# First layer norm with its root on ACT, transposes copied by two engines, matmuls on ones ahead of it, x transposes one V group later

## The chip, the cores and the metric

The kernel runs on one core of one Trainium2 chip. The metric is device microseconds of one execution, without the launch; lower is better.

Engines: PE does matmuls and transposes, PEld is its weight load, DVE is VectorE, ACT is ScalarE, POOL is GpSimd, SP issues the DMAs. A bank is a part of the buffer that PE writes to; in this kernel ACT or DVE copies it out ("evicts" it) before PE fills it again. The granted clock is the share of PE's full clock that the profile records.

## The reference, cut to what matters

The reference is a recurrent memory transformer block followed by a gated MLP with spatial mixing. Only its opening matters here: x is layer-normalized, and from it the projections Q, K and V are taken.

```python
def _layernorm(x, axis=-1, eps=1e-05):
    m = jnp.mean(x, axis=axis, keepdims=True)
    v = jnp.var(x, axis=axis, keepdims=True)
    return (x - m) / jnp.sqrt(v + eps)
# ... in _A_ref, for each of 64 segments of 32 tokens:
    h = jnp.concatenate([mem, xs], axis=1)
    q = jnp.einsum('btd,dhe->bhte', h, Wq)      # D = 512, 32 heads of 128
    k = jnp.einsum('btd,dhe->bhte', h, Wk)
    v = jnp.einsum('btd,dhe->bhte', h, Wv)
# ... main:
x = A_x
h = x + _A_ref(_layernorm(x, axis=-1), ...)
h2 = h + _B_ref(_layernorm(h, axis=-1), ...)
```

## The kernel before: the parts that matter

The program has a start, which projects the rows that every segment needs in advance; a main loop over 64 segments; and the MLP. The change edits the start alone. Its inputs are two 128-row blocks, x0 (`load_xe(0, 0)`) and x1 (`load_xe(1, 1)`), and the three weights, each 4 MB in four quarters. All of the program's DMAs stand in one queue (q1 on the page, 72.26 MB), in this order: x0, x1, four quarters of Wq, some more x, four of Wv, four of Wk.

```python
def ln_stats(j):                         # DVE: statistics; POOL: (var + eps) ** -0.5
    t, tok = xbuf(j); k = j % 3
    dve(... e.bn_stats(out=st1[:, k, :], in_=t) ...)                                     # L364
    dve(... e.bn_aggr(out=mv1[:, k, :], in_=st1[:, k, :]) ...)                           # L365
    pool(... e.tensor_scalar(out=rs1[:, k:k + 1], in0=mv1[:, k, 1:2], scalar1=EPS, op0=ALU.add) ...)   # L366
    pool(... e.tensor_tensor(out=rs1[:, k:k + 1], in0=rs1[:, k:k + 1], in1=mhalf[:, 0:1], op=ALU.pow) ...)  # L368
def ln_apply(j):                         # DVE: (x - mean) * rstd, in place               # L374
def xT(j, bank):                         # PE: four 128x128 transposes into one bank      # L384
def xe_copy(ck, bank):                   # ACT: that bank to hTe[ck]                      # L409
def qkx_mm(ck, i, bank):                 # PE: a group of 16 matmuls on hTe[ck] and Wq/Wk # L426
def vx_mm(ck, n, bank):                  # PE: a V group on Wv                            # L461

act(lambda e: e.preload_act_table_set("natural_log_exp_and_others"))
for j in range(2):
    ln_stats(j)
for j in range(2):
    ln_apply(j)
    xT(j, 6 + j)
    xe_copy(j, 6 + j)
# ... loads of Wv and Wk
def start_group(mm, ev, *a):             # one group into one of 4 banks; evicted by ACT and DVE in turn
    ...
for i in range(8):                       # "Q phase": 16 groups, x0 and x1 in turn
    for ck in range(2):
        start_group(qkx_mm, qkx_evac, ck, i)
    if i == 6:
        for j in range(4, 7):
            ln_stats(j)
        late_consts()
for n in range(8):                       # "V phase": 8 groups of x0
    if n < 3:
        ln_apply(n + 4)
    start_v(0, n)
    if n == 1: xT(4, 6); ring_copy(0, 6)
    if n == 2: xT(5, 7); ring_copy(1, 7)
    if n == 3: xT(6, 6); xe_copy(2, 6); mem0_transpose(7); load_wo(0)
# ... then 8 groups of K, 8 of V (x1), 8 of K; then the main loop
```

The recording layer gives each engine its instructions in this order, and in the traces each engine starts them in it: in after x1 has landed at 4.11 us, but DVE starts its statistics at 6.20, behind x0's half copy (5.99). In the changed kernel the lines move: L374 becomes L378, L384 L388, L409 L413, L426 L431, L436 L441, L461 L466.

The softmax here doesn't subtract the row's maximum and nothing guards it: scores larger than these inputs give would overflow.

## Time and profile before

| what (first trace of before) | us |
|---|---|
| time, median of the first 3 runs | 876.12 (875.36 to 876.2) |
| span of the trace (this execution took 871.85) | 870.1 |
| PE busy | 848.3 |
| first matmul of the Q phase | 7.8 |
| Q phase, to the first V group | 15.8 |
| V phase, to the first K group | 9.08 |
| first matmul of the main loop | 54.19 |

These are lines of the page of before: busy time by engine (us, share of the span, instructions), busy tenths in 40 slices of the span, and the chain that ended last.

```profile
PE 848.3 (97%) x22453; PEld 431.5 (50%) x18869; DVE 502.1 (58%) x1245; ACT 467.4 (54%) x1291; POOL 158.2 (18%) x427
...
PE   6999999999999999999999999999999999999997
...
PE 96%; DVE 2%; issue 1%; DMA 0%; ACT 0%; POOL 0%; SPq 0%
```

PE is the bound, and apart from the last slice, where the work runs out, only its first slice has a hole. This is the timeline of the start of before (start and length in us, engine, line, operation, output<-input, count; in brackets how long the engine had been idle and what ended it):

```profile
4.47 0.22 POOL L366 TENSOR_SCALAR f_rs<-f_mv 128x1 f32<-128x1 f32 x1 [2.91 <-DVE f_mv L365]
...
4.78 0.57 POOL L368 TENSOR_TENSOR f_rs<-f_rs,f_mhalf 128x1 f32<-128x1 f32 x1
...
5.58 0.38 DVE L374 TENSOR_SCALAR f_xn<-f_xn,f_mv,f_rs 128x512 bf16<-128x512 bf16 x1
...
6.01 0.61 PE L384 MATMUL f_ps<-f_ident,f_xn 128*128 128x128 bf16 x4 [6.01 <-DVE f_xn L374]
...
6.66 0.60 ACT L409 ACTIVATE f_hTe<-f_ps 128x512 bf16<-128x512 bf16 x1 [4.59 <-PE f_ps L384]
```

Read alone, this says that PE waits 6 us for the layer norm. It hides the other input of the first group. In the trace's DMA records, the last part of Wq's first quarter lands at 7.67 us, while x0's copy has ended by 7.26. In the second trace of before the PE timeline itself names the DMA:

```profile
6.99 0.61 PE L384 MATMUL f_ps<-f_ident,f_xn 128*128 128x128 bf16 x4 [0.58 <-DVE f_xn L374]
7.90 16.28 PE L426 MATMUL f_ps<-f_hTe,f_arena 128*128 128x128 bf16 x256 [0.31 <-DMA f_arena<-in_A_Wq_dram]
```

Last, PE's wait in the V phase of before, in PE's timeline:

```profile
23.59 1.91 PE L461 MATMUL f_ps<-f_arena,f_hTe 128*32 128x512 bf16 x32
25.98 0.40 PE L384 MATMUL f_ps<-f_ident,f_part 128*128 128x128 bf16 x4 [0.48 <-DVE f_part L374]
```

### The profile page before, as it was taken

Reading aid. Unit: us, or ns where it says so; the run is one execution under the profiler, and the core shown is the slowest. Engines: PE = TensorE matmul, PEld = TensorE weight load, DVE = VectorE, ACT = ScalarE, POOL = GpSimd, SP = SyncE. Lnnn points to the kernel's source line nnn. Section 1 sums busy time; section 2 is a strip of 40 time slices with the busy share of each in tenths; the row PEclk is TensorE's granted clock in tenths of the full one; section 3 lists DMA queues with packets and bytes.
Section 4 is the critical chain, followed back from the end, with each engine's and each line's share of the span. In section 5 each row is a group of like instructions: output and inputs, shape, how many; then the busy total and the mean of one; then the engine's idle time right before and its main releaser. Section 6 shows DMA issues by size and latency. Waiting matters only on the chain.

```text
span 870.1 us, 45443 instructions
## 1 busy us (share of the span) xinstructions
PE 848.3 (97%) x22453; PEld 431.5 (50%) x18869; DVE 502.1 (58%) x1245; ACT 467.4 (54%) x1291; POOL 158.2 (18%) x427
## 2 busy tenths in 40 slices
PE   6999999999999999999999999999999999999997
PEld 6664545544455445554445445555454444444443
DVE  3446666666666666666666666666565554634443
ACT  3446666766666666656666666666666655200000
POOL 1712112121121212121122112121111122100000
PEclk9999999999999999999999999999999999999999
DMA  9972232213031222222241323333221870033001
GB/s 326 379 215 71 76 63 74 66 38 86 25 92 41 67 57 37 72 67 73 62 91 27 81 65 67 95 55 74 51 62 41 209 253 1 0 110 108 26 13 38
DMA packets 114038, 75.22 MB, mean 86 GB/s; under 512 B 70696, under 2 KB 99376, under 8 KB 113840
## 3 DMA queue, kind: packets, MB, share of 16 engines
q1 hardware_dynamic: 113840, 72.26, 30.1%
q8 instruction: 164, 2.69, 1.3%
q14 instruction: 34, 0.28, 0.1%
HBM read 39.46 MB, written 20.58 MB: 69 GB/s over the span
## 4 chain that ended last, share of the span: by engine, by line
PE 96%; DVE 2%; issue 1%; DMA 0%; ACT 0%; POOL 0%; SPq 0%
PE f_ps L280 30%; PE f_ps L660 13%; PE f_ps L281 13%; PE f_ps L1090 11%; PE f_ps L710 3%; PE f_ps L426 3%; PE f_ps L461 3%; PE f_ps L1052 3%; PE f_ps L1083 3%; PE f_ps L1161 3%; PE f_ps L574 3%; PE f_ps L625 3%; PE f_ps L631 1%; PE f_ps L554 1%; PE f_ps L681 1%
## 5 line engine op out<-in xcount | busy, mean ns | idle before, releaser
L280 PE MATMUL f_ps<-f_arena,f_hT 128*32 128x512 bf16 (+1 forms) x5120 | 352.8, 337 | 1.7 <-issue 0.6
L281 PE MATMUL f_ps<-f_arena,f_hT 128*32 128x256 bf16 (+1 forms) x3072 | 214.5, 308 | 0.0
L280 PEld LDWEIGHTS f_ps<-f_arena,f_hT 128*32 128x32 bf16 x5120 | 121.1, 96 | 169.0 <-issue 85.6
L518 ACT ACTIVATE f_Tst<-f_ps 128x512 bf16<-128x512 f32 (+1 forms) x320 | 149.9, 510 | 57.8 <-PE f_ps L280 54.1
L660 PE MATMUL f_ps<-f_arena,f_cT 128*32 128x256 bf16 x4096 | 133.5, 273 | 1.1 <-ACT f_cT L645 1.1
L597 POOL TENSOR_TENSOR f_E_sb<-f_R_sb,f_E_sb 128x64 bf16<-128x64 f32 x128 | 48.1, 376 | 378.2 <-ACT f_R_sb L589 378.2
L526 DVE STREAM_TRANSPOSE f_QT<-f_Tst 128x256 uint32<-128x256 uint32 x128 | 57.0, 446 | 94.9 <-ACT f_Tst L518 94.9
L660 PEld LDWEIGHTS f_ps<-f_arena,f_cT 128*32 128x32 bf16 x4096 | 92.0, 95 | 34.8 <-ACT f_cT L645 21.2
L1090 PE MATMUL f_ps<-f_arena 128*128 128x512 bf16 x448 | 101.3, 379 | 2.5 <-DVE f_arena L1096 1.6
L617 DVE TENSOR_SCALAR f_V_sb<-f_ps 128x512 bf16<-128x512 f32 (+1 forms) x128 | 70.6, 551 | 41.0 <-PE f_ps L280 41.0
L672 ACT ACTIVATE f_part<-f_ps 128x256 bf16<-128x256 f32 x128 | 49.2, 384 | 66.5 <-PE f_ps L660 66.5
L647 DVE TENSOR_SCALAR f_cT<-f_ps 128x160 bf16<-128x160 f32 (+1 forms) x192 | 61.0, 373 | 38.4 <-PE f_ps L631 38.4
L645 ACT ACTIVATE f_cT<-f_ps 128x160 bf16<-128x160 f32 (+1 forms) x192 | 53.0, 348 | 39.4 <-PE f_ps L631 39.4
L1090 PEld LDWEIGHTS f_ps<-f_arena 128*128 128x128 bf16 x448 | 43.6, 98 | 55.9 <-DVE f_arena L1096 2.6
L526 DVE STREAM_TRANSPOSE f_KT<-f_Tst 128x128 uint32<-128x128 uint32 (+1 forms) x192 | 66.0, 356 | 2.7
L585 ACT ACTIVATE f_R_sb<-f_ps 128x160 f32<-128x160 f32 x128 | 38.9, 304 | 33.6 <-PE f_ps L281 26.5
L1096 DVE TENSOR_TENSOR f_arena<-f_ps,f_arena 128x512 f32<-128x512 f32 x28 | 19.3, 690 | 57.8 <-PE f_ps L1090 57.8
L567 ACT ACTIVATE f_E_sb<-f_ps 128x224 bf16<-128x224 f32 x128 | 45.7, 357 | 0.0
L593 DVE TENSOR_TENSOR f_E_sb<-f_R_sb,f_E_sb 128x160 bf16<-128x160 f32 x128 | 44.7, 349 | 0.0
L589 ACT ACTIVATE f_R_sb<-f_R_sb 128x160 f32<-128x160 f32 x128 | 42.6, 333 | 2.0
L710 PE MATMUL f_ps<-f_arena,f_cTx 128*32 128x512 bf16 x512 | 40.5, 380 | 0.0
L280 PE MATMUL f_ps<-f_arena,f_hTe 128*32 128x512 bf16 x512 | 39.0, 382 | 0.0
(105 smaller groups left out, 1024.1 us busy)
## 6 DMA issues: line engine op xcount, KB each, us to landing
wT_d<-f_wst SPq DMA_DIRECT2D x32, 256.0 KB, 2.0
f_arena<-wT_d SPq DMA_DIRECT2D x32, 256.0 KB, 4.8
f_arena<-in_A_Wq_dram SPq DMA_DIRECT2D x4, 1024.0 KB
f_arena<-in_A_Wv_dram SPq DMA_DIRECT2D x4, 1024.0 KB
f_arena<-in_A_Wk_dram SPq DMA_DIRECT2D x4, 1024.0 KB, 15.9
f_arena<-in_A_Wo_dram SPq DMA_DIRECT2D x4, 1024.0 KB
f_Vx<-vext_d SPq DMA_DIRECT2D x128, 32.0 KB
f_xn<-in_A_x_dram SPq DMA_DIRECT2D x16, 128.0 KB, 2.2
```

What stands on the lines that cost most here:

```text
L280: return e.matmul(out, lhsT=lhsT, rhs=rhs, start=start, stop=stop, skip_group_check=True, tile_position=pos)
L281: return e.add_instruction(mybir.InstMatmult(name=nc.get_next_instruction_name(), engine=mybir.EngineType.PE, ins=[e.lower_ap(rhs), e.lowe ...
L518: act(lambda e: e.activation(out=st_.rearrange("p (hp i r) -> p hp i r", i=32, r=2), in_=ps[:, bank, 0:64 * np_].rearrange("p (hp r i) -> ...
L526: dve(lambda e: e.transpose(out=dst, in_=src), reads=tok, writes=[(nm, b, k) for k in halves(b, p0, np_)])
L597: pool(lambda e: e.tensor_tensor(out=ev, in0=rv, in1=ev, op=ALU.mult), reads=[("R", b), ("Ex", b)], writes=[("Ex", b)])
L617: dve(lambda e: e.tensor_scalar(out=dst, in0=src, scalar1=VSC, scalar2=None, op0=ALU.mult), reads=[PB(bank)], writes=tok)
L645: act(lambda e: e.activation(out=dst, in_=src, func=ACT.Copy, scale=UNSC), reads=[PB(PVB[c])], writes=tok)
L647: dve(lambda e: e.tensor_scalar(out=dst, in0=src, scalar1=UNSC, scalar2=None, op0=ALU.mult), reads=[PB(PVB[c])], writes=tok)
L660: pe(lambda e, h=h, g=g, i=i, b=b, c=c: e.matmul(ps[32 * g:32 * g + 32, bank, 0:d1 - d0], lhsT=cTh[:, i, 8:40], rhs=w_o[:, h, d0:d1], star ...
L672: act(lambda e: e.activation(out=part[:, s % 8, d0:d1], in_=ps[:, bank, 0:d1 - d0], func=ACT.Copy), reads=[PB(bank)], writes=[("part", s % ...
L710: pe(lambda e, h=h, g=g, i=8 * qr + bg: e.matmul(ps[32 * g:32 * g + 32, WXB, :], lhsT=cTx[:, rb % 2, i, :], rhs=w_o[:, h, :], start=(i < 4 ...
L1090: pe(lambda e: e.matmul(ps[:, bank, 0:TB], lhsT=z2[:, sc, fb * 128:(fb + 1) * 128], rhs=wTb[tb % 2][:, :, sc, :], start=(sc == 0), stop=(s ...
```

## The change

The intent is to start PE's real work earlier and on a fast clock: a shorter root for x0's layer norm (the root is (var + eps) ** -0.5, here as Ln and Exp on ACT in place of an addition and a power on POOL), its transposes copied in halves by ACT and DVE, 40 matmuls on ones while PE would idle, and x1's layer norm moved behind x0's so that x0 goes first. Separately, the transposes in the V phase come one group later.

```diff
-    def ln_stats(j):
+    def ln_stats(j, on_act=False):
...
+        if on_act:
+            act(lambda e: e.activation(out=rs1[:, k:k + 1], in_=mv1[:, k, 1:2], func=ACT.Ln, bias=EPS), ...)
+            act(lambda e: e.activation(out=rs1[:, k:k + 1], in_=rs1[:, k:k + 1], func=ACT.Exp, scale=-0.5), ...)
+            return
...
-    for j in range(2):
-        ln_stats(j)
-    for j in range(2):
-        ln_apply(j)
-        xT(j, 6 + j)
-        xe_copy(j, 6 + j)
+    for _ in range(40):
+        pe(lambda e: e.matmul(ps[:, 5, 0:128], lhsT=onesrc[:, 0:128], rhs=onesrc[:, 0:128], start=True, stop=True), ...)
+    ln_stats(0, True)
+    ln_apply(0)
+    xT(0, 6, (0, 1))
+    xT(0, 7, (2, 3))
+    act(lambda e: e.activation(out=hTe[:, 0, 0:2, :], in_=psb[:, 6, 0:256]..., func=ACT.Copy), ...)
+    dve(lambda e: e.tensor_copy(out=hTe[:, 0, 2:4, :], in_=psb[:, 7, 256:512]...), ...)
+    ln_stats(1, True)
+    ln_apply(1)
...
             start_group(qkx_mm, qkx_evac, ck, i)
+            if ck == 0 and i == 0:
+                xT(1, 1)
+                xe_copy(1, 1)
...
-        if n == 1:
+        if n == 2:
             xT(4, 6)
...                                     # likewise n == 2 -> 3 and n == 3 -> 4
```

The rest of the diff splits the dependency token of `hTe` into two halves.

More of the change, by code (lines that the diff above doesn't have):

```diff
@@ L365, in ln_stats @@
         dve(lambda e: e.bn_aggr(out=mv1[:, k, :], in_=st1[:, k, :]), reads=[("st1", k)], writes=[("mv1", k)])
+        if on_act:
+            act(lambda e: e.activation(out=rs1[:, k:k + 1], in_=mv1[:, k, 1:2], func=ACT.Ln, bias=EPS), reads=[("mv1", k)], writes=[("rs1", k)])
+            act(lambda e: e.activation(out=rs1[:, k:k + 1], in_=rs1[:, k:k + 1], func=ACT.Exp, scale=-0.5), reads=[("rs1", k)], writes=[("rs1", k)])
+            return
         pool(lambda e: e.tensor_scalar(out=rs1[:, k:k + 1], in0=mv1[:, k, 1:2], scalar1=EPS, scalar2=None, op0=ALU.add),
@@ L379, in ln_inplace, with xT @@
         ln_apply(j)
-    def xT(j, bank):
+    def xT(j, bank, dcs=range(DC)):
         t, tok = xbuf(j)
-        for dc in range(DC):
+        for dc in dcs:
             pe(lambda e, dc=dc: e.transpose(out=psb[:, bank, dc * 128:(dc + 1) * 128], in_=t[:, dc * 128:(dc + 1) * 128],
@@ L393, in x_flip @@
         sp(lambda e: e.dma_start(xs_d[i], t), reads=rd, writes=[("xs", i)])
-        sp(lambda e: e.dma_start_transpose(out=dst, in_=xs_d[i]), reads=[("xs", i)], writes=[tok])
+        sp(lambda e: e.dma_start_transpose(out=dst, in_=xs_d[i]), reads=[("xs", i)], writes=tok)
     def ring_fill(rb):
@@ L408, in xe_copy @@
         src = psb[:, bank, 0:512].rearrange("p (dc c) -> p dc c", dc=DC)
-        act(lambda e: e.activation(out=hTe[:, ck % 3, :, :], in_=src, func=ACT.Copy), reads=[PB(bank)], writes=[("hTe", ck % 3)])
+        act(lambda e: e.activation(out=hTe[:, ck % 3, :, :], in_=src, func=ACT.Copy), reads=[PB(bank)],
+            writes=[("hTe", ck % 3, 0), ("hTe", ck % 3, 1)])
     def mem0_transpose(bank):
@@ L427, in qkx_mm @@
                                                          rhs=hTe[:, ck % 3, dc, :], start=(dc == 0), stop=(dc == DC - 1)),
-                   reads=[("hTe", ck % 3), ("W", mi, q // 2)], writes=[PB(bank)])
+                   reads=[("hTe", ck % 3, dc // 2), ("W", mi, q // 2)], writes=[PB(bank)])
     def qkx_evac(ck, i, bank, eng="act"):
@@ L445, in qkx_rows @@
                                           dc == 0, dc == DC - 1, (0, 32 * c)),
-               reads=[("hTe", ck % 3), ("W", mi, 2 * b), ("W", mi, 2 * b + 1)], writes=[PB(bank)])
+               reads=[("hTe", ck % 3, dc // 2), ("W", mi, 2 * b), ("W", mi, 2 * b + 1)], writes=[PB(bank)])
     def qkx_flip(ck, mi, r, b, bank):
@@ L462, in vx_mm @@
                                                        start=(dc == 0), stop=(dc == DC - 1), tile_position=(0, 32 * c)),
-                   reads=[("hTe", ck % 3), ("W", 2, n // 2)], writes=[PB(bank)])
+                   reads=[("hTe", ck % 3, dc // 2), ("W", 2, n // 2)], writes=[PB(bank)])
     def vx_evac(ck, n, bank, eng="act"):
@@ L758, in fast_path @@
     act(lambda e: e.preload_act_table_set("natural_log_exp_and_others"))
-    for j in range(2):
-        ln_stats(j)
-    for j in range(2):
-        ln_apply(j)
-        xT(j, 6 + j)
-        xe_copy(j, 6 + j)
+    for _ in range(40):
+        pe(lambda e: e.matmul(ps[:, 5, 0:128], lhsT=onesrc[:, 0:128], rhs=onesrc[:, 0:128], start=True, stop=True), reads=["onesrc"], writes=[PB(5)])
+    ln_stats(0, True)
+    ln_apply(0)
+    xT(0, 6, (0, 1))
+    xT(0, 7, (2, 3))
+    act(lambda e: e.activation(out=hTe[:, 0, 0:2, :], in_=psb[:, 6, 0:256].rearrange("p (dc c) -> p dc c", dc=2), func=ACT.Copy),
+        reads=[PB(6)], writes=[("hTe", 0, 0)])
+    dve(lambda e: e.tensor_copy(out=hTe[:, 0, 2:4, :], in_=psb[:, 7, 256:512].rearrange("p (dc c) -> p dc c", dc=2)),
+        reads=[PB(7)], writes=[("hTe", 0, 1)])
+    ln_stats(1, True)
+    ln_apply(1)
     for mi in (2, 1):
@@ L797, in fast_path @@
         start_v(0, n)
-        if n == 1:
+        if n == 2:
             xT(4, 6)
             ring_copy(0, 6)
-        if n == 2:
+        if n == 3:
             xT(5, 7)
             ring_copy(1, 7)
-        if n == 3:
+        if n == 4:
             xT(6, 6)
@@ L985, in fast_path @@
         if j4 == 1 and 2 <= rb + 2 < RB:
-            late.append(lambda rb=rb: (ln_apply(0), x_flip(0, rb, xn[:, 1, :].rearrange("p (dc c) -> p dc c", dc=DC), ("xn", 1))))
+            late.append(lambda rb=rb: (ln_apply(0), x_flip(0, rb, xn[:, 1, :].rearrange("p (dc c) -> p dc c", dc=DC), [("xn", 1)])))
         if s == 2:
@@ L989, in fast_path @@
         if s == 3:
-            late.append(lambda: (ln_apply(7), x_flip(7, RB, hTe[:, 0, :, :], ("hTe", 0))))
+            late.append(lambda: (ln_apply(7), x_flip(7, RB, hTe[:, 0, :, :], [("hTe", 0, 0), ("hTe", 0, 1)])))
         if j4 == 1 and rb >= 2:
```

## The prediction

> **What bounds the kernel now.** The chain of waits gives PE 96% of the span, and PE is busy 848.3 of 870.1 us. The change touches only the first 33 us. There the timeline shows three losses:
> - PE starts at 6.01 us with transposes of x0; the first projection matmul (L426) starts at 7.80.
> - PE starts slow: L426 matmuls are 107 ns apart until 10.75 us and 56 ns after it. 28 of them are slow, about 28 x 51 ns = 1.4 us. [...]
> - In the V phase PE waits 0.5 us (25.5 to 26.0) for DVE's layer norm of part.
>
> **The hidden floor.** x0's transposes are copied by 7.26 us, but the trace's DMA landings put the first quarter of Wq at 7.67, and PE's wait for it ends at 7.75. So L426 already starts on the weights, not on the layer norm. Later quarters leave little room: Wk's first lands at 31.54, its users start at 32.67.
>
> **What the change does.** The POOL pair (0.22 + 0.57 us and gaps, 4.47 to 5.35) becomes Ln and Exp on ACT, estimated at 0.2 us each from the 0.19 us of a 128x32 ACTIVATE: saves about 0.4 us. With fast transposes and two half copies (about 0.4 us, estimated from the 0.60 us copy) x0's hTe is ready near 6.3 instead of 7.26. That is off the critical path: Wq lands near 7.7.
>
> The 40 matmuls on ones fill about 1.1 to 5.4 us (40 x 107 ns) and should warm PE. Near 764 us a 1.8 us idle stretch leaves later matmuls at 216 ns, so idling to 7.7 should not cool it. Then the first group takes 0.9 us (7.8 to 8.7), not 1.6.
>
> But x1 is now late: its statistics stand behind DVE's half copy (about 6.35), so it is normalized near 8.3 and transposed after the first group, near 8.9. Its copy (0.60) stands on ACT behind the first group's eviction (0.74 us, 8.9 to 9.65), so the second group starts near 10.3 and issues its last matmul near 11.2; before it was 10.93. So a new PE wait eats the warm clock's 1.4 us, and the Q phase ends 0.0 to 0.4 us later.
>
> V phase: x transposes a group later remove the 0.5 us wait: 9.08 us (23.59 to 32.67) becomes about 8.5. Wk (31.54) then just does not bind.
>
> The rest is PE-bound and merely shifts. [...]a 0.86 us "issue" gap at 61.2 may come or go.
>
> **Sum.** -1.4 (clock) + 1.6 (new wait) - 0.55 (V phase) = about -0.35 us: 875.7 us (8 in 10: 873.8 to 877.2). Chances: faster by over 2% 0.01, within 2% 0.98, slower by over 2% 0.01.
>
> **What would show it.** First L426 still near 7.8: floor right. 56 ns apart from there: warming right. A PE gap of over 1 us before the second L426 group, released by ACT's hTe copy: new wait right. No wait of L384 on DVE near 25 us: V phase right. Start of the main loop (54.19 before) near 53.9.
>
> **What would make it wrong.** PE cooling again in the idle stretches (about 0.9 us slower); weights landing earlier (up to 1 us more gain, until Wk binds); [...]run-to-run spread (0.8 us before).

What the first trace of before shows: PE has work from 7.20 us, and its matmuls are 107 ns apart until 10.75 and 56 ns after it; later PE idles for 1.80 us ahead of L1041 (765.73), and the matmuls that follow are 216 ns apart, as before the idle stretch.

## More of the kernel before

The windows view gives busy time with counts, and the granted clock, in any stretch. For before, up to 10.77 us and after it (columns: stretch and length; PE, PEld, DVE, ACT, POOL busy with counts; clock, DMA share, GB/s):

```profile
7.36:10.77 3.41, 3.41 (x33) 3.17 (x32) 0.00 (x0) 1.34 (x2) 0.00 (x0) 1.00 1.05 394
10.77:14.18 3.41, 3.41 (x64) 3.41 (x63) 1.46 (x2) 1.05 (x2) 0.00 (x0) 1.00 1.05 386
```

In the first stretch 33 matmuls are under way, in the second 64: one every 107 ns, then one every 56 ns. The clock column says 1.00 for both, because this trace's clock record begins only with the first switch, at 10.77; before it one has to look at the matmuls.

## The result, and the profile after

Six runs of the changed kernel: median 876.96 us (875.3 to 879.15); before, in the same rounds and those of the first measurement: 875.74 (872.86 to 876.2). A ratio is the mean time of one kernel's fast runs over that of the other's in the same rounds, so it is not quite the ratio of these medians. It is 1.0023, with a 95% interval of 1.0001 to 1.0045: within 2%, and slower by some 2 us (0.1 to 3.9) where 0.4 us faster was foretold. The median lies inside the foretold range, but before was itself quicker in these rounds: set against the 876.12 from which the prediction started, the ratio stands for 878.1. A second measurement (below) gave 1.0036.

The timeline of the start of after, first trace:

```profile
1.07 4.45 PE L765 MATMUL f_ps<-f_onesrc 128*128 128x128 bf16 x40 [1.07 <-POOL f_onesrc L328]
...
4.37 0.20 ACT L367 ACTIVATE f_rs<-f_mv 128x1 f32<-128x1 f32 x1 [2.30 <-DVE f_mv L365]
4.60 0.20 ACT L368 ACTIVATE f_rs<-f_rs 128x1 f32<-128x1 f32 x1
...
5.32 0.63 PE L388 MATMUL f_ps<-f_ident,f_xn 128*128 128x128 bf16 x4
...
5.99 0.29 DVE L772 COPY f_hTe<-f_ps 128x256 bf16<-128x256 bf16 x1 [0.74 <-PE f_ps L388]
6.20 0.68 DVE L364 BATCH_NORM_STATS2 f_st<-f_xn 128x6 f32<-128x512 bf16 x1
...
8.15 1.05 PE L431 MATMUL f_ps<-f_hTe,f_arena 128*128 128x128 bf16 x16 [2.20 <-DMA f_arena<-in_A_Wq_dram]
...
9.04 0.39 PE L388 MATMUL f_ps<-f_ident,f_xn 128*128 128x128 bf16 x4
...
9.24 0.74 ACT L441 ACTIVATE f_arena<-f_ps 128x512 bf16<-128x512 f32 x1 [1.67 <-PE f_ps L431]
9.84 0.58 ACT L413 ACTIVATE f_hTe<-f_ps 128x512 bf16<-128x512 bf16 x1
10.47 2.58 PEld L431 LDWEIGHTS f_ps<-f_hTe,f_arena 128*128 128x128 bf16 x25 [1.22 <-ACT f_hTe L413]
```

Four things stand there. The root takes two times 0.20 us on ACT, and x0's two half copies end near 6.3 us, about 1 us before the 7.26 of before. The first group gains nothing from it: it starts at 8.15, after 2.2 us of idling, when Wq has landed (8.01 in this run). The first group is fast: 16 matmuls and four transposes start between 8.15 and 9.2. And then PE waits for x1: its statistics came after x0's half copy on DVE, its transposes after the first group on PE, its copy after that group's eviction on ACT.

The V phase is as hoped; in PE's timeline of after there is no wait ahead of L388:

```profile
25.34 2.77 PE L466 MATMUL f_ps<-f_arena,f_hTe 128*32 128x512 bf16 x48
28.05 0.40 PE L388 MATMUL f_ps<-f_ident,f_part 128*128 128x128 bf16 x4
```

But it begins at 25.34, against 23.59 before. The windows view of after shows why the wait for x1 is not the whole of it:

```profile
3.14:6.55 3.41, 2.81 (x27) 2.49 (x24) 1.85 (x5) 0.79 (x3) 0.00 (x0) 1.00 1.00 305
6.55:9.96 3.41, 1.28 (x20) 1.13 (x20) 0.92 (x3) 1.13 (x4) 0.00 (x0) 1.00 1.05 400
9.96:13.38 3.42, 2.91 (x28) 2.91 (x29) 0.73 (x1) 0.46 (x2) 0.00 (x0) 0.50 1.05 387
13.38:16.79 3.41, 3.41 (x64) 3.41 (x62) 1.01 (x2) 1.50 (x2) 0.00 (x0) 1.00 1.06 369
```

The warm-up got the fast clock, at 6.55. The next 3.41 us held PE busy for only 1.28 us, and the clock was halved for the 3.41 us after them, in which 28 matmuls are counted where the following stretch counts 64. Before, which never warms up early, has its 28 slow matmuls while it waits for nothing; after has 27 slow ones anyway, later, and the wait on top.

### The profile page after: what moved, and what is told of

Same layout as the page of the kernel before. It is cut to its first block, busy times and chain, and to the rows that moved or that the text cites. A ratio compares the mean times of both kernels' runs of the same rounds, so it can differ in the third digit from the quotient of the medians.

```text
span 875.9 us, 45517 instructions
## 1 busy us (share of the span) xinstructions
PE 855.7 (98%) x22486; PEld 437.4 (50%) x18909; DVE 502.7 (57%) x1246; ACT 467.9 (53%) x1295; POOL 156.8 (18%) x423
## 4 chain that ended last, share of the span: by engine, by line
PE 96%; DVE 1%; issue 1%; DMA 1%; ACT 0%; SPq 0%; POOL 0%
PE f_ps L280 30%; PE f_ps L665 13%; PE f_ps L281 13%; PE f_ps L1104 11%; PE f_ps L431 3%; PE f_ps L466 3%; PE f_ps L715 3%; PE f_ps L1066 3%; PE f_ps L1097 3%; PE f_ps L579 3%; PE f_ps L1175 3%; PE f_ps L630 3%; PE f_ps L636 1%; PE f_ps L559 1%; PE f_ps L686 1%
```

## The experiments

**Two readings to tell apart.** Theory T: after loses because the clock that the 40 matmuls bought is taken back while PE idles. Theory X: it loses because x1 comes late. Besides, the first pair of traces differed by 5.8 us of span, of which only 1.2 us stood at the start of the main loop; so theory P (the 80 added PE instructions move the main loop's stalls) and its rival N (noise of single runs) had to be told apart too.

All traces, in us. "Slow" counts Q-phase matmuls recorded 107 ns apart instead of 56. The time from the first K group to the main loop was 21.52 us (to 0.01) in every trace.

| trace | first group | Q phase | slow | V phase | loop starts | loop start to L1041* | L1041* to end |
|---|---|---|---|---|---|---|---|
| before | 7.81 | 15.78 | 28 | 9.08 | 54.19 | 711.6 | 104.4 |
| before again | 7.91 | 16.21 | 37 | 9.08 | 54.72 | 711.7 | 104.9 |
| before, third | 7.68 | 16.96 | 51 | 9.08 | 55.24 | 712.6 | 104.5 |
| after | 8.15 | 17.20 | 27 | 8.53 | 55.41 | 714.5 | 106.0 |
| after again | 7.69 | 18.59 | 55 | 8.54 | 56.34 | 711.0 | 104.3 |
| after, third | 7.58 | 18.36 | 50 | 8.54 | 56.00 | 712.9 | 104.4 |
| no warm | 8.12 | 17.97 | 43 | 8.54 | 56.16 | 709.9 | 104.3 |
| warm only | 7.83 | 14.38 | 0 | 9.57 | 53.30 | 712.3 | 106.0 |
| after, filled | 8.08 | 15.84 | 0 | 8.54 | 53.98 | 714.0 | 106.5 |
| x1 early | 8.01 | 16.01 | 33 | 8.53 | 54.08 | 713.1 | 104.5 |
| V shift only | 8.33 | 16.74 | 47 | 8.54 | 55.13 | 713.1 | 104.5 |
| pool root | 8.04 | 19.37 | 70 | 8.54 | 57.47 | 714.0 | 104.7 |
| pool root again | 7.76 | 17.38 | 31 | 8.54 | 55.21 | 713.5 | 104.8 |
| x1 early, filled | 7.76 | 14.38 | 0 | 9.94 | 53.60 | 713.9 | 104.3 |

*L1041 is the one matmul of the finiteness check in the MLP, at 765.74 us in before; its line differs in the other kernels.

### 1 and 2. Both kernels against themselves

No edit. Five rounds each, on one chip with 3 and 4.

> The kernel before, unchanged, against itself. It tells how far two traces and two times of the same program differ. Theory P[...]: the time from the first main-loop matmul to the start of the last phases repeats within 0.5 us of the first trace of before (54.19 us to about 684.7 us), and the single stalls (0.86 us near 61.2, 0.97 us near 558.9) stand at the same places. Rival N (run-to-run noise): loop time differs by 1 us or more and the stalls move. Both: ratio 1.000, main loop starts at 54.2 +-0.3 us.

> The changed kernel once more. Main loop starts at 55.4 +-0.5 us if PE again falls back to the slow clock after the first group; about 54.1 if this time it stays fast. Theory P: loop time about 1.8 us longer than before's, stalls (1.14 us near 689) at the same places as in the first trace of after. Rival N: loop time anywhere, stalls elsewhere. [...] Ratio to before 1.001 to 1.004.

Before against itself: ratio 1.0000 (0.9985 to 1.0015). After: 1.0036 (1.0020 to 1.0052), median 875.73 against 872.40 us. So the loss is real, and the noise of five rounds is some 1.3 us either way. Main loop starts at 54.72 and 56.34, both later than foretold (54.2 +-0.3 and 55.4 +-0.5). From the loop's start to L1041 before took 711.6 and 711.7 us, after 714.5 and then 711.0, a spread of 3.5 us within one program: these traces speak for N, not P. The stall near 61 us stood there in two traces of before (0.86 and 0.92 us) and not in the third.

In this trace of after the clock was halved for two stretches, from 9.02 to 15.85 us. The 40 matmuls (4.45 us) bought 3.41 us of fast clock, of which PE used 1.51:

```profile
2.20:5.61 3.41, 3.41 (x35) 3.41 (x33) 1.29 (x3) 0.41 (x2) 0.00 (x0) 1.00 0.84 240
5.61:9.02 3.41, 1.51 (x24) 1.19 (x21) 1.49 (x4) 1.03 (x4) 0.00 (x0) 1.00 1.05 400
9.02:12.43 3.41, 2.41 (x23) 2.42 (x24) 0.49 (x1) 0.94 (x2) 0.00 (x0) 0.50 1.05 387
12.43:15.85 3.42, 3.42 (x35) 3.42 (x33) 0.73 (x2) 0.74 (x1) 0.00 (x0) 0.50 1.05 379
```

The wait for x1 held PE to 2.41 of 3.41 us in the third stretch, and in the fourth the clock was still 0.50.

### 3. The change without its 40 matmuls

```diff
-    for _ in range(40):
-        pe(lambda e: e.matmul(ps[:, 5, 0:128], lhsT=onesrc[:, 0:128], ...
```

> The change without its 40 matmuls on ones. Theory W (the warm-up is partly used: the first group, 16 matmuls, runs at 56 instead of 107 ns): first group 0.8 us longer than in after, x1's copy and the second group 0.8 us later, main loop starts near 56. Rival (the slow clock between 9.6 and 13.0 us in after was caused by warming too early and then idling, so the warm-up costs as much as it gives): main loop starts at 55.4 or earlier[...].

Ratio 1.0014 (0.9998 to 1.0029), loop start 56.16, 43 slow matmuls. That lies between the three traces of after (55.41, 56.00, 56.34): inside after, the 40 matmuls neither gain nor lose anything at the start of the main loop that these traces can show. The expectation that they save 0.8 us was a comparison with 55.41, the luckiest of the three traces. The whole times say something else: in the same rounds no warm took 873.47 us on average and after 875.37. These 1.9 us (0.0 to 3.8, an estimate from the spread of 5 and 6 runs) are just clear of noise, and the starts don't explain them.

### 4. Before with the 40 matmuls alone

```diff
+    for _ in range(40):
+        pe(lambda e: e.matmul(ps[:, 5, 0:128], lhsT=onesrc[:, 0:128], ...
     for j in range(2):
         ln_stats(j)
```

> The kernel before with the 40 matmuls on ones alone (x0 and x1 both normalized and transposed ahead of the first group, as before). Theory W: L426 matmuls 56 ns apart from the first, which still starts at 7.7 to 8.0 us because Wq's first quarter lands then; no wait before the second group; 1.4 us gained there, of which the weights of K take back some 0.4 (they land at 31.5): main loop starts near 53.2. Rival (PE always falls back after a warm-up that is followed by idling): slow again from about 9.6 for 3.4 us, main loop starts at 54 to 54.5. Theory P of the main loop: this kernel has as many more PE instructions as after, so its loop stalls should look like after's (1 to 2 us longer than before's); rival N: no such likeness.

The same 40 matmuls work here: no slow matmul at all, Q phase 14.38 us, loop start 53.30 as foretold. Here x1 is ready in time. PE was busy for 1.89 of 3.41 us in the stretch around the first group's start, and in the next one 65 matmuls were under way (64 in before's first fast one):

```profile
5.39:8.80 3.41, 1.89 (x28) 1.45 (x27) 0.85 (x3) 1.19 (x2) 0.86 (x2) 1.00 1.05 398
8.80:12.21 3.41, 3.41 (x65) 3.41 (x63) 1.34 (x2) 1.48 (x2) 0.00 (x0) 1.00 1.05 389
```

The ratio to before is 1.0005 (0.9991 to 1.0020). The loop starts 1.4 us ahead of the mean of before (54.72), but by this interval at most 0.8 us of that arrives in the whole time; the traces don't show why. From the loop's start to L1041 it took 712.3 us, within the 711.6 to 712.6 of before, so here too nothing speaks for P.

### 5. The change with PE kept busy

```diff
     xT(0, 7, (2, 3))
+    for _ in range(30):                 # the same matmul on ones
...
                 xT(1, 1)
+                for _ in range(12):
```

> The changed kernel with 30 more matmuls on ones between x0's transposes and the first group and 12 more between x1's transposes and the second group, so that PE has work in its two idle stretches. x1 stays as late as in after. Theory T (after loses by PE's clock falling back, because it idles after the warm-up): no slow L431 matmul at all (27 and 55 in the two traces of after, 107 ns apart), the wait of about 1 us before the second group stays, main loop starts at 54.0 +-0.4 us (55.4 and 56.3 in after). Rival X (the late x1 alone costs it): still above 55, since x1 is as late as before.

Theory T foretold 54.0; the loop starts at 53.98, without one slow matmul. The wait for x1 is still there, partly filled with ones:

```profile
5.55 1.84 PE L771 MATMUL f_ps<-f_onesrc 128*128 128x128 bf16 x30
8.07 1.05 PE L431 MATMUL f_ps<-f_hTe,f_arena 128*128 128x128 bf16 x16 [0.68 <-DMA f_arena<-in_A_Wq_dram]
8.96 0.39 PE L388 MATMUL f_ps<-f_ident,f_xn 128*128 128x128 bf16 x4
9.19 0.83 PE L806 MATMUL f_ps<-f_onesrc 128*128 128x128 bf16 x12
10.41 13.57 PE L431 MATMUL f_ps<-f_hTe,f_arena 128*128 128x128 bf16 x240 [0.40 <-ACT f_hTe L413]
```

With the clock fast throughout, its Q phase of 15.84 us against 14.38 in warm only prices the late x1 alone: 1.46 us. Ratio 0.9992 (0.9976 to 1.0009).

### 6. The change with x1 ahead of the first group

```diff
     ln_stats(0, True)
+    ln_stats(1, True)
     ln_apply(0)
...
-    ln_stats(1, True)
     ln_apply(1)
+    xT(1, 1)
+    xe_copy(1, 1)
...                                     # and these two calls no longer stand after the first group
```

> The changed kernel with x1's statistics, normalization, transposes and copy ahead of the first group, as in before; nothing else undone. Theory X: no wait before the second group, and with it PE has work without a break from the first group on[...]. If it stays fast the main loop starts at 53.3 us, held there by the first quarter of Wk landing near 31.7; if it falls back, near 54.3. Theory T alone (idle time before the first group, not x1, makes the clock fall): slow matmuls for 3.4 us again, 54 or later.

The wait before the second group is gone, yet 33 matmuls are slow and the loop starts at 54.08, near the 54.3 foretold for the case that the clock falls. So the two causes are separate. The stretch ahead of the fall has no gap longer than 0.71 us in it:

```profile
5.42:8.83 3.41, 1.72 (x24) 1.31 (x24) 0.98 (x4) 1.39 (x4) 0.00 (x0) 1.00 1.05 404
8.83:12.24 3.41, 3.41 (x36) 3.41 (x33) 0.73 (x1) 0.74 (x1) 0.00 (x0) 0.50 1.05 387
```

With 1.72 us busy here the clock was halved next; with 1.89 in warm only it was not. Ratio 1.0005 (0.9988 to 1.0022).

### 7. Before with the V shift alone

```diff
-        if n == 1:
+        if n == 2:
             xT(4, 6)
...                                     # n == 2 -> 3, n == 3 -> 4
```

> The kernel before with the x transposes one V group later and nothing else. The wait of 0.48 us of L384 on DVE near 25.5 us goes, the V phase (9.08 us in both traces of before) takes 8.55 us, main loop starts at 53.65 to 54.2 us (54.19 and 54.72 in before). Ratio within 0.2% of 1. Rival (the wait only moves to a later place, such as bank or DVE evictions): V phase stays near 9.0.

V phase 8.54 us, against 9.08 in all three traces of before: this part gives 0.54 us, as foretold. The loop start missed its range (55.13) because in this run x0's transposes began at 6.52, the first group at 8.33, and 47 matmuls were slow, all of it ahead of what the edit moves. The ratio, 0.9976 (0.9959 to 0.9993), is more than the trace accounts for; its near end is 0.6 us.

### 8 and 9. The change with the roots back on POOL

```diff
-    ln_stats(0, True)
+    ln_stats(0)
...
-    ln_stats(1, True)
+    ln_stats(1)
```

> The changed kernel with both roots back on POOL (add and power) and all else as in after. Floor theory: x0's copies end near 6.7 instead of 6.3, still ahead of Wq's first quarter (7.6 to 8.0), so the first group starts 0.13 us after that landing as in after; x1 is normalized 0.4 us later (8.4) but is transposed only after the first group (9.0): main loop starts at 55.4 to 56.4 as in after. Rival (the root is on the critical path): first group 0.4 us later relative to the landing, or the second group 0.4 to 0.8 us later.

> The same kernel as the pool root run, whose trace fell in a case where the warm-up never took (70 slow matmuls, main loop at 57.5). If that was [...]not the root: this time the first group is fast, 20 to 55 matmuls are slow later, main loop at 55.4 to 56.5. If the root on POOL itself prevents it (by 0.5 us more idle time before the transposes): 70 slow again, 57.5.

In both traces what ends PE's wait before the first group is Wq's DMA (1.60 us of idling up to 8.03, 1.38 up to 7.76), as in after (2.20 up to 8.15). The root on ACT is worth nothing on the critical path. In the first trace the warm-up never took: 70 matmuls were slow, the first group's among them (16 in 1.86 us). The second shows that the root on POOL does not by itself prevent it: 31 slow, loop start 55.21. The timed runs agree: the granted clock is 0.999 in the traced one, which had no early fast clock to lose, and 0.993 to 0.995 in the other three. Ratio of the first: 1.0018 (1.0001 to 1.0035).

### 10. x1 early and PE kept busy

```diff
-    for _ in range(40):
+    for _ in range(46):
...                                     # x1 as in 6; 10 more after x0's transposes, 6 after x1's
```

> The changed kernel with x1 ahead of the first group (as in the run x1 early) and with 46, 10 and 6 matmuls on ones before x0's transposes, after them and after x1's. If the two causes add (late x1: about 1 us; clock falling back: 1.2 to 2.4 us), no slow L431 matmul, no wait before the second group, Q phase ends at 22.3 us, and the main loop starts at 53.3 us, held there by the first quarter of Wk (31.6 to 31.9), so PE waits about 0.8 us for it. Rival: after with filling alone (54.0) is already all there is, then 54.0. Ratio to before 0.997 to 1.000, not clear of noise.

No slow matmul, no wait, Q phase 14.38 us. Then the next bound shows, in PE's timeline:

```profile
28.19 2.99 PE L466 MATMUL f_ps<-f_arena,f_hTe 128*32 128x512 bf16 x48
32.08 4.12 PE L431 MATMUL f_ps<-f_hTe,f_arena 128*128 128x128 bf16 x71 [0.90 <-DMA f_arena<-in_A_Wk_dram]
```

The V phase runs into Wk's first quarter (PE waits 0.90 us for it, to 32.08), so the loop starts at 53.60 and not at 53.3. This is the best of both kernels' parts: 1.1 us ahead of the mean of before (54.72) at the loop's start, 2.3 ahead of after's (55.92). In whole times it is not clear of noise against before: 873.59 against 874.30 us, ratio 0.9989 (0.9975 to 1.0003).

### 11 and 12. A third trace of each

> A third trace of the changed kernel: main loop starts between 55.3 and 56.4 us (or 57.5 if the warm-up does not take), a wait of about 1 us before the second group, at least 20 slow L431 matmuls after it.

> A third trace of before: main loop starts between 54.1 and 55.0 us, 28 to 47 slow matmuls at the start[...], V phase 9.1 us.

After: loop start 56.00, 50 slow; this time the clock was fast from 4.13 and fell at 7.54, just before the first group, so even that was slow. Before: 55.24, a little above its range, 51 slow, V phase 9.08.

### What the windows show

In the first trace of after the clock record switches at 6.55, 9.96, 13.37, 771.13, 774.55 and 873.53 us: the steps are 3.413 us, or 222 and 29 times that. Before's stretch at full clock, 10.77 to 867.52, is 251 times 3.413 us. The half-clock stretch of x1 early lasted 3.41 us, those of after again and of after, third, twice that. The first switch moves from run to run: 6.55, 5.61 and 4.13 us in the three traces of after. What sets its moment the traces don't show.

These are the stretches of 3.41 us that were looked up, by the clock in them and in the next one, with PE's busy time as the windows view counts it:

- Full clock, halved in the next stretch: 1.18 us (after, third), 1.28 (after), 1.51 (after again), 1.72 (x1 early), and near L1041 1.35 (after) and 1.39 (after, filled).
- Full clock, kept: 1.89 us (warm only), 2.22 and 2.51 (before, near L1041), 2.73 and 3.01 (after, filled), 3.26 (x1 early, filled).
- Half clock, still half in the next stretch: 2.41 us (after again), 2.52 (after, third). Half clock, full in the next: 2.91 (after), and 3.41 to 3.42 (after again, after, third, x1 early).

Two stretches in the last 10 us kept the fast clock at busy shares of 0.49 (no warm) and 0.46 (pool root again), below the 0.50 (1.72 us) that lost it in x1 early. So the view's busy time does not sort them all, and these single stretches of this program give no limit that could be carried elsewhere.

Such switches go with most of the differences in the last column of the table. At L1041 PE idles for 1.8 us in both kernels. In the first trace of before that time was split between two stretches (2.22 and 2.51 us busy) and the clock stayed at 1.00. In the first trace of after, in warm only and in after, filled, one stretch held nearly all of it (1.35, 1.35 and 1.39 us busy). In after and in after, filled, the record shows the clock halved for the next 3.41 us; in all three the end took 1.1 to 2.2 us longer than in the others. It happened in 3 of 14 traces and belongs to no part of the change.

## Why the prediction was wrong

In the Q phase the time is the sum of three terms, in every one of the 14 traces within 0.06 us: 14.38 us, plus 0.051 us for each slow matmul (107 less 56 ns), plus 1.46 us if x1 is late. For after: 14.38 + 27 x 0.051 + 1.46 = 17.22 (measured 17.20); after again: 18.65 (18.59).

- **The floor: right.** "L426 already starts on the weights." First groups at 7.68 to 7.91 us in before and 7.58 to 8.15 in after, the means 7.80 and 7.81. The faster root and the half copies brought nothing; putting the root back on POOL cost nothing.
- **The new wait: right.** Foretold 1.6 us, measured 1.46.
- **The V phase: right.** Foretold 0.55 us, measured 0.54.
- **The clock: wrong, and this is the step that failed.** The sum has "-1.4 (clock)", from "a 1.8 us idle stretch leaves later matmuls at 216 ns, so idling to 7.7 should not cool it". Measured: 28, 37 and 51 slow matmuls in before, mean 39; 27, 55 and 50 in after, mean 44. That is +0.3 us, in place of -1.4. The timed runs show the lost clock too: the granted clock is 0.993 to 0.998 in 13 runs of after (mean 0.9950) and 0.996 to 1.000 in 33 of before in the later rounds (mean 0.9988). One half-clock stretch of 3.41 us is worth 0.002 of it (half of 3.41 us in some 873), so by this estimate after lost about two of them more in each run; the slow start ahead of the first switch is not in this record (it reads 1.00 up to 10.77 us in before, with matmuls 107 ns apart). The evidence was misread: the idle stretch near 764 us left the clock alone in the first trace of before, where PE was busy for 2.22 and 2.51 us of the two stretches that it fell into, but not in that of after, where one stretch held it and PE was busy for 1.35. A gap that kept the clock once said nothing of a start in which PE idles for 2.20 us and then again for 1.05. The prediction argued from the length of one gap; x1 early lost the clock with no gap above 0.71 us. It did name the loss of the clock under "what would make it wrong", and put it at 0.9 us of cost; it should have been the main case.
- **"The rest is PE-bound and merely shifts": right as far as shown.** K to loop took 21.52 us in all traces; the loop up to L1041 took 711.6 to 712.6 us in before and 711.0 to 714.5 in after.

The sum as measured at the start of the main loop: -0.54 (V) + 1.46 (x1) + 0.3 (clock) = +1.2 us, which is the difference of the means, 55.92 - 54.72. Three traces of each kernel are few for the clock's term: the slow matmuls run from 28 to 51 in before and from 27 to 55 in after. The measured ratios, 1.0023 and 1.0036, stand for 2.0 us (0.1 to 3.9) and 3.1 us (1.7 to 4.5). The first agrees with the 1.2 us; the second interval begins above it, so part of that loss may stand outside the start.

What stays open: the main loop takes 709.9 to 714.5 us to L1041 in these traces without an order by kernel, and no run here tells what makes it differ. That spread is larger than everything the change does. Open is also what the 40 matmuls do to whole times where PE idles after them: warm only starts its loop 1.4 us ahead of before and is not quicker as a whole, and after is 1.9 us behind no warm though their loops start within 0.3 us of each other (55.92 and 56.16). The two kernels that keep PE busy agree with their starts: 0.7 us ahead of before in both numbers for after, filled, and 1.1 (start) and 1.0 (whole) for x1 early, filled, with some 1.3 us of noise on each whole time.

## What to carry to other kernels

Before moving work ahead of a first matmul, look up when each of its inputs lands; the releaser in a timeline is only the last of them, and 0.4 us behind x0's copy there was a DMA here (7.26 and 7.67 us in before). In this program the fast clock that a warm-up of PE bought was kept until real work was dense where PE was then busy for 1.89 of 3.41 us (warm only), 2.73 (after, filled) or 3.26 (x1 early, filled), and was lost where it was busy for 1.18 to 1.51 (after) or 1.72 (x1 early). So trace the time between a warm-up and the real work too, and try filling it. And when one operand is hurried, trace what was pushed behind it on each engine: x1, moved back, cost 1.46 us, while the hurry gained nothing.
